# Attention 0 ahead of gate/up 0, and gate/up and projections in 64-row tile pairs with a shifted copy of x

## Chip, cores and metric

The kernel runs on one core of a Trainium2 chip. The metric is the device time of one execution in microseconds (us). The engines are called as in the profile: PE (matmuls; PEld its weight loads), DVE, ACT (functions such as exp, and copies), POOL, and SP, which issues most DMAs in one queue.

## What is computed

The input x has 2048 rows of 448 columns in bf16. Cut to what matters:

```python
xn = layernorm(x)
q, k, v = xn @ wq, xn @ wk, xn @ wv            # 16 heads of 28
for s in range(4):                             # segments of 512 rows
    p     = softmax(q_s @ k_s.T * 28**-0.5 + causal_mask)
    a_mem = phi(q_s) @ M / (phi(q_s) @ z + 1e-6)          # phi(t) = elu(t) + 1
    o_s   = g * a_mem + (1 - g) * (p @ v_s)               # g = sigmoid(beta), by head
    M, z  = M + phi(k_s).T @ v_s, z + phi(k_s).sum(rows)
s = o @ wo
g = silu((gelu(xn @ w_gate) * (xn @ w_up)) @ w_down)      # hidden width 1792
out = x + s * g
```

## The kernel before

`fast_path` (L339 to L1374) builds a list of operations, each with its engine, duration, buffers and dependencies. `arrange` (L276) then fixes the order on every engine once, when the program is built: it takes the operation that can start soonest, and among those near it the one of lowest priority number. Three tables steer it. `ORDER` (L273) is the sequence of stages; `PRIO` (L87 to L257) overrides priorities by name; `STEP` (L258 to L272) says behind which score step of its segment's attention an operation may stand. On the chip every engine runs its row in that order and waits for semaphores. SP's row is served in order too: a DMA that waits for its data holds those behind it.

The work is cut into segments of 512 rows and into stages. A(s) is attention of segment s, G(s) gate/up of segment s, D3 the last down-projection. Before, the sequence is G0, A0, A1, G1, A2, G2, A3, G3, D3.

*Layer norm and transposition.* x is normalised on DVE, ACT and POOL, and turned so that its 448 columns lie on partitions: three chunks of 128 and one of 64. Segment 0's two copies, a centred one for its projections and the normalised one for gate/up 0, are turned by PE (`turned_by_pe`, L590, transposes at L596), those of the other segments by transposing DMAs (L685).

*Projections.* A `Unit` is one block of 128 rows by one of q, k, v: three full 128-row matmuls and one of 64 rows (`product`, L711; L714 in the profile). `visit` (L768) collects the 64-row matmuls of several units: one unit uses the low 64 rows of the PE array, the next the high 64, so two run side by side. Results are copied out of PSUM by ACT or DVE (L750 to L754); q and k are turned by DMA (L763) into qT and kT. phi (L816) is exp on ACT (L826) and elementwise work on POOL and DVE.

*Attention.* Ten score steps per segment (L985) use 32-row tiles, four heads at a time. exp on ACT (L1000) reads one or two PSUM banks, POOL masks the diagonal blocks (L1011), P·V (L1047) uses tiles 32 columns wide. The denominators go through small DMAs: collected (L886), reshaped (L917), inverted, spread again (L926, L931), and multiplied in by POOL (L909, L948, L956). `read` (L898) and `update` (L860) are the linear memory. Between score steps PE gets other work: projections of a later segment, the down-projection of the segment before (L1155), and `wo` (L1185). The residual is L1176.

*Gate/up.* For each of 14 blocks of 128 hidden columns there are six full matmuls (L1089) and two of 64 rows (L1104), the latter collected over four blocks (`VISITS`): 

```python
VISITS = (((), (0, 1)), ((2, 3), (4, 5)), ((6, 7), (8, 9)), ((10, 11), (12, 13)))
for i, w in enumerate((wg_sb, wu_sb)):
    for c in range(NC3):                                   # NC3 = 3 chunks of 128 rows
        nc.tensor.matmul(out=bf[fc].ap(i), lhsT=w[:, c, fc * P:(fc + 1) * P], ...)
r = slice(i * HALF, (i + 1) * HALF)                        # gate low, up high
nc.tensor.matmul(out=bf[fc].ap(i), lhsT=wh_sb[r, fc * P:(fc + 1) * P], ...)
```

gelu is ACT's (L1114), the product with up DVE's (L1119); the result is hT, input of the down-projection. `guard` (L1239) checks a bound on the weights. `general_path` isn't run.

Of the kernel before, what the change touches and what calls it, by code (L numbers as in the profile page):

```python
# [1737 lines left out]
```

## Time and profile before

| what | value |
|---|---|
| time, median of 3 runs | 229.91 us (229.48 to 230.01) |
| span of the profiled execution | 228.8 us, 1.1 us below the median of the runs |
| PE busy | 219.1 us, 96% of the span |
| DVE, ACT, POOL busy | 152.5, 152.8, 129.2 us |
| granted clock of PE | full, 1.00 in nearly every stretch |
| DMA traffic | 25.09 MB, 110 GB/s on the mean |

The stages in that execution: the first gate/up matmul starts at 16.75 us, A0's first score at 39.29, A1's at 64.21, G1 at 89.39, A2 at 112.16, G2 at 139.76, A3 at 162.53, G3 at 187.11, the last down-projection at 209.99; PE's last large matmul ends at 223.1.

How to read the profile: a line such as `L1104 ... x4` is a group of four instructions of source line 1104; `ps` and `pp` are PSUM banks (single ones and pairs). "x3" behind a DMA transpose counts blocks. In the chain of waits each row is a piece of the path that ends last: its start, its length, and what ran. Of a stage, such a row tells which engine set its pace.

### The profile page before, as it was taken

The numbers are of one execution on the slowest core, as the hardware profiler recorded it, in microseconds if no ns is written. First come the engines' busy times: TensorE is split into PE (matmuls) and PEld (weight loads), VectorE is DVE, ScalarE is ACT, GpSimd is POOL, SyncE is SP. The second block draws the span as 40 slices with busy tenths as digits, with TensorE's granted clock in tenths as the row PEclk, the third lists the DMA queues.
The fourth block names the chain that finished last, engine by engine and source line by source line (L and its number), as shares of the span: only waits on it lengthen the run. The fifth ranks groups of instructions, "written<-read, shape, count | busy, mean of one in ns | idle before, by whom it ended". The sixth has DMA issues, their size and how long they took to land.

```text
span 228.8 us, 4476 instructions
## 1 busy us (share of the span) xinstructions
PE 219.1 (96%) x1570; PEld 95.8 (42%) x1570; DVE 152.5 (67%) x287; ACT 152.8 (67%) x212; POOL 129.2 (56%) x221
## 2 busy tenths in 40 slices
PE   7899999889999999999999999999999999999991
PEld 2444433334444444344444444444444434444570
DVE  3699998766955796674775587863836463548262
ACT  4699735999899679433788898443878875336020
POOL 8501400579579599602699989853198487604400
PEclk9999999999999999999999999999999999999999
DMA  6999559954436682326702122272400018133011
GB/s 211 230 354 253 103 129 251 251 116 92 52 72 72 177 130 53 80 52 191 197 20 59 35 70 62 66 195 84 114 1 4 11 44 227 34 103 99 4 40 47
DMA packets 44707, 25.09 MB, mean 110 GB/s; under 512 B 30808, under 2 KB 40856, under 8 KB 44680
## 3 DMA queue, kind: packets, MB, share of 16 engines
q1 hardware_dynamic: 43704, 24.05, 45.1%
q10 hardware_dynamic: 976, 0.71, 1.0%
q8 instruction: 13, 0.21, 0.4%
q14 instruction: 14, 0.11, 0.2%
HBM read 16.00 MB, written 2.98 MB: 83 GB/s over the span
## 4 chain that ended last, share of the span: by engine, by line
PE 83%; ACT 7%; DMA 4%; issue 2%; DVE 2%; ACTq 0%
PE ps L1089 16%; PE pp L1089 16%; PE ps L1155 14%; PE ps L714 11%; ACT pt L1000 6%; PE pp L985 5%; PE ps L1185 4%; PE ps L1047 3%; PE pp L1104 3%; PE ps L1104 3%; DMA wv_sb<-in_A_wv_dram 2%; PE pp L1155 2%; DMA qT<-e 2%; PE ps L898 1%; PE pp L714 1%
## 5 line engine op out<-in xcount | busy, mean ns | idle before, releaser
L1000 ACT ACTIVATE pt<-pp 128x1024 bf16<-128x1024 f32 x75 | 73.3, 1037 | 11.7 <-PE pp L985 9.8
L1011 POOL TENSOR_SCALAR_AFFINE_SELECT pt<-pt 128x256 bf16<-128x256 bf16 x128 | 54.0, 446 | 26.8 <-ACT pt L1000 24.4
L1155 PE MATMUL ps<-wd_sb,hT 128*128 128x448 bf16 x182 | 39.1, 354 | 0.4 <-DVE qs L750 0.4
L1114 ACT ACTIVATE gl<-pp 128x512 bf16<-128x512 f32 x28 | 15.8, 595 | 29.0 <-PE pp L1104 23.3
L1155 PEld LDWEIGHTS <-hT 128*128 128x128 bf16 x210 | 18.8, 98 | 20.0 <-issue 4.8
L1119 DVE TENSOR_TENSOR hT<-gl,pp 128x512 bf16<-128x512 bf16 x28 | 18.4, 682 | 12.3 <-ACT gl L1114 12.3
L1119 DVE TENSOR_TENSOR hT<-gl,ps 128x512 bf16<-128x512 bf16 x28 | 18.7, 677 | 10.7 <-ACT gl L1114 8.2
L1114 ACT ACTIVATE gl<-ps 128x512 bf16<-128x512 f32 x28 | 16.6, 597 | 13.2 <-PE ps L1089 6.7
L1089 PEld LDWEIGHTS <-wu_sb 128*128 128x128 bf16 x168 | 16.5, 98 | 20.0 <-issue 0.3
L1089 PEld LDWEIGHTS <-wg_sb 128*128 128x128 bf16 x168 | 14.9, 98 | 22.6 <-issue 6.8
L909 POOL TENSOR_TENSOR om<-om,rb 128x512 f32<-128x512 f32 x12 | 14.9, 1267 | 16.4 <-DMA rb<-rdr 16.4
L714 PEld LDWEIGHTS <-xnT 128*128 128x128 bf16 (+1 forms) x192 | 15.0, 96 | 20.9 <-issue 10.5
L1089 PE MATMUL ps<-xnT,wg_sb 128*128 128x512 bf16 x84 | 22.8, 380 | 0.0
L1089 PE MATMUL pp<-xnT,wg_sb 128*128 128x512 bf16 x84 | 22.8, 380 | 0.0
L1089 PE MATMUL ps<-xnT,wu_sb 128*128 128x512 bf16 x84 | 22.7, 379 | 0.1
L1089 PE MATMUL pp<-xnT,wu_sb 128*128 128x512 bf16 x84 | 22.7, 379 | 0.0
L956 POOL TENSOR_TENSOR oT<-oa,om 128x512 bf16<-128x512 f32 x12 | 16.0, 1341 | 11.0 <-DVE oa L953 11.0
L985 PE MATMUL pp<-qT,kT 32*128 32x512 bf16 (+3 forms) x238 | 17.3, 301 | 1.9 <-ACT pt L1000 1.8
L831 POOL TENSOR_SCALAR e<-e 128x896 bf16<-128x896 bf16 (+1 forms) x12 | 12.8, 1069 | 10.9 <-ACT e L826 10.9
L646 POOL TENSOR_TENSOR rs<-rs,nhalf 128x1 f32<-128x1 f32 (+1 forms) x7 | 6.1, 882 | 16.6 <-DVE rs L641 16.6
L883 DVE COPY oa<-ps 128x512 f32<-128x512 f32 x16 | 11.0, 684 | 6.0 <-PE ps L1047 5.5
L1176 POOL TENSOR_TENSOR oo<-sg,x_sb 128x448 bf16<-128x448 f32 x12 | 12.4, 1035 | 2.5 <-DVE sg L1196 2.5
(121 smaller groups left out, 326.0 us busy)
## 6 DMA issues: line engine op xcount, KB each, us to landing
rb<-rdr SPq DMA_DIRECT2D x28, 256.0 KB
out_dram<-oo SPq DMA_DIRECT2D x15, 112.0 KB
wd_sb<-in_B_w_down_dram SPq DMA_DIRECT2D x2, 784.0 KB
x_sb<-in_A_x_dram SPq DMA_DIRECT2D x3, 448.0 KB
rdr<-dc SPq DMA_DIRECT2D x28, 32.0 KB
wg_sb<-in_B_w_gate_dram SPq DMA_DIRECT2D x2, 384.0 KB
wu_sb<-in_B_w_up_dram SPq DMA_DIRECT2D x2, 384.0 KB
wg_sb<-in_B_w_gate_dram SPq DMA_DIRECT2D x1, 576.0 KB
```

Source lines behind the costliest of these rows:

```text
L714: nc.tensor.matmul(out=self.bank.ap()[:, 0:D], lhsT=self.xT.ap()[r, c, n * P:(n + 1) * P], rhs=self.w[r, c, :], **kw)
L831: o = gps(f"mi{nm}{s}{half}", n / 1024, lambda: nc.gpsimd.tensor_scalar(out=t(), in0=t(), scalar1=1.0, scalar2=0.0, op0=ALU.min, op1=ALU.max),
L909: oU[s, g, 1] = t, gps(f"sm{s}{g}", 1.22, lambda t=t, r=r: nc.gpsimd.tensor_tensor(out=t.ap(), in0=t.ap(), in1=r.ap(), op=ALU.mult), deps= ...
L956: oT[s][1].append(gps(f"cb{s}{g}", 1.22, lambda g=g, t=t, tm=tm: nc.gpsimd.tensor_tensor(out=dst.ap()[:, g, :], in0=t.ap(), in1=tm.ap(), o ...
L985: nc.tensor.matmul(out=S2[i // 2].ap(i % 2)[:, c0:c0 + n], lhsT=kT[s][0].ap()[r, g, kb * P:(kb + 1) * P], rhs=qT[s][0].ap()[r, g, kb * P:L ...
L1000: nc.scalar.activation(out=dst, in_=src, func=ACT.Exp, scale=scale)
L1011: nc.gpsimd.affine_select(out=v, in_=v, pattern=[[0, 2], [1, P]], compare_op=ALU.is_ge, fill=0.0, base=0, channel_multiplier=-1)
L1089: nc.tensor.matmul(out=bf[fc].ap(i), lhsT=w[:, c, fc * P:(fc + 1) * P], rhs=xT.ap()[:, c, :], start=begins and c == 0, stop=not begins and ...
L1104: nc.tensor.matmul(out=bf[fc].ap(i), lhsT=wh_sb[r, fc * P:(fc + 1) * P], rhs=xT.ap()[r, NC3, :], start=fc in begins, stop=fc in ends)
L1114: a = act(f"ge{s}{fc}", L, lambda: nc.scalar.activation(out=gl.ap(), in_=bf[fc].ap(0), func=ACT.Gelu_apprx_tanh), func="gelu", deps=[o], a ...
L1119: nc.vector.tensor_tensor(out=hT[s][0].ap()[:, fc, :], in0=gl.ap(), in1=bf[fc].ap(1), op=ALU.mult), deps=[a] + held,
L1155: nc.tensor.matmul(out=bank.ap()[:, 0:D], lhsT=hT[s][0].ap()[:, fc, b * P:(b + 1) * P], rhs=wd_sb[:, fc, :], start=(fc == 0), stop=(fc == ...
```

## The change

*Sequence.* `ORDER` becomes A0, G0, A1, G1, A2, G2, A3, G3, D3. Down-projection and residual of segment s - 1 now stand in A(s) for s = 1, 2, 3, and `combine` (the output of attention) of segment s behind G(s). Projections of segment 1 stand in A0; q and k of segment 2 in A1, its v in A2; q and k of segment 3 in A2, its v in A3. The tables `PRIO` and `STEP` are new; `STEP` now counts through all 40 score steps.

*64-row tiles throughout.* The 448 rows are cut into seven half chunks of 64 instead of 3 x 128 + 64. Gate weights lie in partitions 0 to 63 and up weights in 64 to 127 of one tensor, q and k weights likewise, and v weights twice. A block of gate/up is 14 matmuls of 64 rows, gate (low) and up (high) in turn, each into its own PSUM bank. A projection is a `pair` of units, 14 matmuls. `VISITS`, `full` and `halves` go.

*A shifted copy of x.* The low tile needs every half chunk of x in partitions 0 to 63, the high one in 64 to 127. What lies on the other side is read from a copy xS with the halves swapped. `swapped` makes it by two DMAs from on-chip memory to on-chip memory of 196 KB each, once per segment for the projections and once for gate/up; for the projections of segment 0 it comes from seven transposes by PE per block instead of four.

*Segment 0 and 1.* q and one block of k of segment 0 are turned by PE (20 transposes in all) and copied by ACT or DVE, the other three k blocks by DMA. The normalised x of segment 1 is turned by PE instead of DMA, that of segment 0 for gate/up 0 by DMA instead of PE.

*Buffers.* k, kT and v of segment 0 live in the down weights' tensor wd_sb, which is loaded after A0; qT of segment 0 lives in hT. x of segment 3 shares the tile of segment 0. The guard's squares go over the q/k tensor, behind A0.

The diff, cut to its core:

```diff
-ORDER = {"G0": 0, "A0": 1, "A1": 2, "G1": 3, "A2": 4, "G2": 5, "A3": 6, "G3": 7, "D3": 8}
+ORDER = {"A0": 0, "G0": 1, "A1": 2, "G1": 3, "A2": 4, "G2": 5, "A3": 6, "G3": 7, "D3": 8}
...
-        wg_sb = const.tile([P, NC3, F], BF16, name="wg_sb")
-        wu_sb = const.tile([P, NC3, F], BF16, name="wu_sb")
-        wh_sb = const.tile([P, F], BF16, name="wh_sb")
+        wgu_sb = const.tile([P, NH, F], BF16, name="wgu_sb")
...
+        def swapped(s, use, pr):
+
+            t, (xT, xd) = Buf(xS_p), xnT[s]
+            lo = dma(f"xs{use}{s}l", 196, lambda: nc.sync.dma_start(
+                out=t.ap()[side[0]], in_=xT.ap()[side[1], 0:NC3, :]), deps=list(xd), prio=pr, acq=[t], uses=[xT])
+            hi = dma(f"xs{use}{s}h", 196, lambda: nc.sync.dma_start(
+                out=t.ap()[side[1]], in_=xT.ap()[side[0], 1:NC3 + 1, :]), deps=list(xd), after=[lo], prio=pr, uses=[t, xT])
+            xS[s, use] = t, [lo, hi]
+
+        def chunk(xT, xt, h, hi):
+
+            if hi:
+                t, c = (xT, NC3) if h == 0 else (xT, h // 2) if h % 2 else (xt, h // 2 - 1)
+            else:
+                t, c = (xt if h % 2 else xT), h // 2
+            return t.ap()[side[hi], c, :]
+
+        turn_of = (0, 2, 4, 6, 1, 3, 5), (1, 3, 5, 0, 2, 4, 6)
...
-                r, n = slice(0, P) if c < NC3 else side[self.n % 2], self.n
-                nc.tensor.matmul(out=self.bank.ap()[:, 0:D], lhsT=self.xT.ap()[r, c, n * P:(n + 1) * P],
-                                 rhs=self.w[r, c, :], **kw)
+                h, n = turn_of[self.hi][k], self.n
+                nc.tensor.matmul(out=self.bank.ap()[:, 0:D], lhsT=chunk(self.xT, self.xt, h, self.hi)[:, n * P:(n + 1) * P],
+                                 rhs=self.w[side[self.hi], h, :], start=k == 0, stop=k == NH - 1)
...
+                    for k in range(NH):
                         for i in range(2):
+                            h = turn_of[i][k]
+                            nc.tensor.matmul(out=bf.ap(i), lhsT=wgu_sb[side[i], h, cols], rhs=chunk(xT, xt, h, i),
+                                             start=k == 0, stop=k == NH - 1)
+                o = prev = pe(f"gu{s}{fc}", [L] * 7, mm, mode="r64", deps=xd + xe + gu_in[fc],
+                              after=[prev or att.get("sc_end")], prio=at(ph, fc) + 0.5, acq=[bf], uses=[xT, xt])
...
-            d = max(s - 1, 0)
...
             if s > 0:
                 for b in range(NB):
-                    finish(d, b, at(A(s), 90 + 10 * b))
+                    down(s - 1, b, at(A(s), 12 + 24 * b))
+                for b in range(NB):
+                    finish(s - 1, b, at(A(s), 90 + 10 * b))
```

What stands on PE at the first scores of attention 0, before (kT and qT are keys and queries of segment 0, turned; L714 is a projection of segment 1):

```order
L1089 MATMUL ps_95<-xnT_98,wu_sb 128x512
L985 LDWEIGHTS kT_102
L985 MATMUL pp_91<-qT_100,kT_102 128x512
L985 LDWEIGHTS kT_102
L985 MATMUL pp_91<-qT_100,kT_102 128x512
L985 LDWEIGHTS kT_102
L985 MATMUL pp_90<-qT_100,kT_102 128x512
L985 LDWEIGHTS kT_102
L985 MATMUL pp_90<-qT_100,kT_102 128x512
L714 LDWEIGHTS xnT_99
```

And after (wd_sb holds the keys, hT the queries; L826 is the last projection of segment 0, with the shifted copy xS; L696 turns segment 1's x):

```order
L826 LDWEIGHTS xS_96
L826 MATMUL ps_88<-wv_sb,xS_96 128x448
L1097 LDWEIGHTS wd_sb
L1097 MATMUL pp_86<-hT,wd_sb 128x512
L1097 LDWEIGHTS wd_sb
L1097 MATMUL pp_86<-hT,wd_sb 128x512
L1097 LDWEIGHTS wd_sb
L1097 MATMUL pp_87<-hT,wd_sb 128x512
L1097 LDWEIGHTS wd_sb
L1097 MATMUL pp_87<-hT,wd_sb 128x512
L696 LDWEIGHTS xn_92
```

The scores moved from behind gate/up 0 to right behind the projections of segment 0.

PE at the start of gate/up 1, before (L1185 is the last `wo` of segment 0):

```order
L1185 MATMUL ps_92<-wo_sb,oT_126 128x448
L1104 LDWEIGHTS wh_sb
L1104 MATMUL ps_93<-xnT_99,wh_sb 128x512
L1104 LDWEIGHTS wh_sb
L1104 MATMUL ps_95<-xnT_99,wh_sb 128x512
L1104 LDWEIGHTS wh_sb
L1104 MATMUL pp_90<-xnT_99,wh_sb 128x512
L1104 LDWEIGHTS wh_sb
L1104 MATMUL pp_90<-xnT_99,wh_sb 128x512
L1089 LDWEIGHTS wg_sb
L1089 MATMUL ps_93<-xnT_99,wg_sb 128x512
```

And after:

```order
L1097 MATMUL pp_86<-qT_98,kT_100 128x128
L1195 LDWEIGHTS wgu_sb
L1195 MATMUL ps_88<-xnT_94,wgu_sb 128x512
L1195 LDWEIGHTS wgu_sb
L1195 MATMUL ps_90<-xnT_94,wgu_sb 128x512
L1195 LDWEIGHTS wgu_sb
L1195 MATMUL ps_88<-xnT_94,wgu_sb 128x512
L1195 LDWEIGHTS wgu_sb
L1195 MATMUL ps_90<-xnT_94,wgu_sb 128x512
```

Instead of four 64-row matmuls followed by full ones, 64-row ones follow one another, low and high in turn, and gate/up 1 stands behind the last scores of attention 1.

SP's row ahead of gate/up 0, after the change (xnT_95 is the normalised x of segment 0 and its second copy xS_96 the one that gate/up 0 reads; xnT_94 and xS_97 belong to segment 1):

```order
L870 DMA_TRANSPOSE wd_sb<-wd_sb 128x4x128 x3
L709 DMA xS_97<-xnT_94 64x1536
L711 DMA xS_97<-xnT_94 64x1536
L592 DMA wgu_sb<-in_B_w_gate_dram 64x7x512
L801 DMA_TRANSPOSE xnT_95<-xn_92 128x4x128 x2
L658 DMA wo_sb<-in_A_wo_dram 28x4x448 x3
L592 DMA wgu_sb<-in_B_w_up_dram 64x7x512
L801 DMA_TRANSPOSE xnT_95<-xn_92 128x4x128 x2
L870 DMA_TRANSPOSE qT_98<-qs 128x4x128
L592 DMA wgu_sb<-in_B_w_gate_dram 64x7x768
L870 DMA_TRANSPOSE qT_98<-e_103 128x4x128
L709 DMA xS_96<-xnT_95 64x1536
```

Before, the queue held at this place the transposes of k, q and x and the loads of x, wo and wd, and gate/up 0, which reads segment 0's x as PE turned it, waited for none of them.

More of the change, by code (lines that the diff above doesn't have):

```diff
@@ L493, in load, with weight @@
             return o
-        def weight(eng, name, dst, ap):
-            kb = ap.shape[1] / 4
-            return [load(eng, name, dst[:, 0:NC3, :], ap[0:NC3 * P, :].rearrange("(c p) n -> p c n", p=P), 3 * kb)
-                    ] + [load(eng, f"{name}{i + 2}", dst[i * HALF:(i + 1) * HALF, NC3, :], ap[NC3 * P:D, :], kb / 2, 110.0)
-                         for i in range(2)]
+        side = slice(0, HALF), slice(HALF, P)
+        def weight(eng, name, dst, hi, ap, parts):
+            v = ap.rearrange("(c p) n -> p c n", p=HALF)
+            return [load(eng, f"{name}{k or ''}", dst[side[hi], c, :], v[:, c, :], len(range(*c.indices(NH))) * ap.shape[1] / 8, 300.0)
+                    for k, c in enumerate(parts)]
         x0 = [load(e, f"x0{lo}", xs[0][:, lo:hi, :], x_v[0][:, lo:hi, :], 112 * (hi - lo))
@@ L503, in fast_path @@
         x_in = {0: [x0[0], x0[2], x0[1], x0[1]]}
[L504 to L508 removed]
+        even, odd = slice(0, NH, 2), slice(1, NH, 2)
+        wq_in, wk_in = [], []
+        for k in range(2):
+            wq_in += weight("ACT", f"wq{k}", wqk_sb, 0, A_wq, [(even, odd)[k]])
+            wk_in += weight("SP", f"wk{k}", wqk_sb, 1, A_wk, [(odd, even)[k]])
+        wqk_in = wq_in + wk_in
+        x_in[1] = [load("SP", "x1", xs[1][:], x_v[1], 448)] * NB
+        wv_in = weight("SP", "wvl", wv_sb, 0, A_wv, [slice(0, NH)]) + weight("SP", "wvh", wv_sb, 1, A_wv, [slice(0, NH)])
+        x_in[2] = [load("SP", "x2", xs[2][:], x_v[2], 448)] * NB
         gu_in = []
@@ L546, in fast_path @@
                 t[:, :, :, Dh:Dh + 1], 1.0), after=[o], prio=-389 + 300 * i))
-        ones_in = fill("POOL", "ones", 0.1, 20, ones[:], 1.0)
+        ones_in = [fill("POOL", f"on{i}{j}", 0.1, 20, ones[side[i], j:j + 1], float(i == j)) for i in range(2) for j in range(2)]
         bd_in = []
@@ L1124, in hidden @@
                 hT[s][1].append(m)
[L1125 to L1135 removed]
+            hT[s].append(prev)
             att["g_end"], att["gelu_end"] = prev, a
@@ L1241, in guard, with square, sums @@
             sq = [Buf(pt_p), Buf(pt_p)]
-            for n in range(2 * (NC3 + 1)):
-                i, c = divmod(n, NC3 + 1)
-                to, r, d = sq[n // 4], slice(0, P) if c < NC3 else side[0], Dh
-                w = (wk_sb if i else wq_sb)[r, c, :]
-                def square(n=n, to=to, r=r, d=d, w=w):
-                    nc.scalar.activation(out=to.ap()[r, n % 4, 0:H * d], in_=w, func=ACT.Square)
-                def sums(i=i, c=c, n=n, to=to, r=r, d=d):
+            for n in range(NH):
+                to = sq[n // 4]
+                def square(n=n, to=to):
+                    nc.scalar.activation(out=to.ap()[:, n % 4, 0:D], in_=wqk_sb[:, n, :], func=ACT.Square)
+                def sums(n=n, to=to):
@@ L1255, in guard, with both @@
                         after=[a], prio=pr, acq=[] if n % 4 else [to], uses=[to] if n % 4 else [])
-                last.append(dve(f"rq{n}", H * d / 960 + 0.05, sums, deps=[a], prio=pr, uses=[to]))
+                last.append(dve(f"rq{n}", D / 960 + 0.05, sums, deps=[a], prio=pr, uses=[to]))
             bank = Buf(B_, ONE)
-            o = pe("nrm", [128], lambda: nc.tensor.matmul(
-                out=bank.ap()[0:1, 0:2 * (NC3 + 1) * H], lhsT=ones[:],
-                rhs=um[:, 0, :], start=True, stop=True), deps=last + [ones_in], prio=pr,
-                acq=[bank])
+            def both():
+                for i in range(2):
+                    nc.tensor.matmul(out=bank.ap()[0:1, i * NH * H:(i + 1) * NH * H], lhsT=ones[:, i:i + 1],
+                                     rhs=red, start=True, stop=True)
@@ L1328, in fast_path @@
         last_block(at(8, 40))
-        for o in later:
-            o.after.append(xnT[1][1][-1])
+        for t, o in o_users:
+            t.users.append(o)
+        x_in[3][0].deps += [ops_by[f"fa0{b}"] for b in range(NB)]
         for s in range(NSEG):
```

417 lines of the change are left out of this document (188 added, 229 removed), and 457 rows, old and new, of tables (PRIO, STEP).

## The prediction

> **What bounds the kernel now.** I read the page's head first, then the busy time of each engine in eleven stretches cut at the starts of the stages, then the chain of waits, and last the timelines of ScalarE (ACT) and of the DMA queue (SPq) around attention 0. Page, engine totals and the chain's shares:
>
> ```profile
> span 228.8 us, 4476 instructions
> PE 219.1 (96%) x1570; PEld 95.8 (42%) x1570; DVE 152.5 (67%) x287; ACT 152.8 (67%) x212; POOL 129.2 (56%) x221
> PE 83%; ACT 7%; DMA 4%; issue 2%; DVE 2%; ACTq 0%
> ```
>
> TensorE (PE) is busy for 96% of the span and carries 83% of the chain. The other engines matter only where PE has a hole. The stretches show where (columns: stretch, its length, busy time of PE, PEld, DVE, ACT, POOL, granted clock, DMA share, GB/s):
>
> ```profile
> 0.00:16.75 16.75, 14.53 (x90) 7.08 (x92) 11.02 (x33) 11.72 (x26) 8.12 (x33) 1.00 0.89 262
> 16.75:39.30 22.55, 22.48 (x118) 8.90 (x114) 21.39 (x51) 14.91 (x25) 3.66 (x3) 1.00 0.86 185
> 39.30:64.20 24.90, 22.98 (x210) 9.77 (x211) 19.70 (x43) 23.30 (x29) 16.41 (x34) 1.00 0.66 126
> 64.20:89.40 25.20, 25.19 (x236) 11.09 (x237) 18.11 (x31) 21.57 (x27) 21.58 (x39) 1.00 0.59 104
> 89.40:112.20 22.80, 22.80 (x132) 9.21 (x132) 13.94 (x22) 10.84 (x17) 10.94 (x13) 1.00 0.49 127
> ...
> 223.10:228.80 5.70, 0.58 (x14) 0.43 (x11) 1.24 (x5) 0.56 (x2) 0.00 (x0) 0.92 0.18 47
> ```
>
> They are the start, gate/up 0, attention 0 (39.30), attention 1 (64.20), gate/up 1 (89.40), and the tail behind the last matmuls. From 64.20 on PE has no hole; before it, PE is idle at the start and in attention 0, and 5.7 us at the end hold almost no PE work. The clock is full, so it is no term. The pieces of the chain give PE's paces (start, us, what):
>
> ```profile
> 9.09 0.22 PE ps L596 x4
> 22.47 0.54 PE ps L1104 x4
> 23.01 0.43 PE pp L1104 x4
> 43.17 0.81 issue
> 43.98 5.35 ACT pt L1000 x8
> ...
> 57.55 3.62 DMA qT<-e
> 61.27 1.06 ACT e L826
> 74.17 0.33 PE pp L985 x8
> 81.64 0.66 PE ps L1047 x16
> 98.35 2.59 PE ps L1089 x12
> ```
>
> Twelve full 128-row gate/up matmuls take 2.59, so 0.216 us each. Four 64-row ones (L1104), which run as two pairs, take 0.43 when others of their kind stand ahead: a pair costs 0.216, as much as one full matmul. The same four take 0.54 right behind a full one: a change of tile shape costs 0.54 - 0.43 = 0.11 us. Eight 32-row score matmuls take 0.33, sixteen of P·V 0.66, four transposes 0.22 (0.055 each). In attention 0 the chain leaves PE: exp (L1000) for 5.35 us, then a transposing DMA and phi.
>
> **The change part by part.**
>
> *Tile shapes.* By the order of PE's instructions the work in columns stays: gate/up was 336 full matmuls and 56 pairs, 392 units, and is 784 halves, 392 pairs; projections were 144 + 24 = 168 units and are 168 pairs of 448 columns. What goes is changes of shape. I counted them in that order: 156 before, 112 after. Gate/up 1 to 3 have 10, 10 and 9 before and 3 each after; the rest is spread over gate/up 0 (7 to 3) and the attentions. That is 44 x 0.108 (the 0.11 above, unrounded) = **-4.75 us**. Added are 32 transposes: 20 for queries and keys of segment 0, 12 for shifted and later x: 32 x 0.055 = **+1.8 us**. Costing every instruction so, PE's sums are 213.8 before and 210.8 after. Before, 228.8 - 5.7 - 213.8 leaves 9.3 us in which PE did not progress.
>
> These are 4.8 at the start (16.75 against a sum of 11.96), 0.6 in gate/up 0 (22.55 against 21.96), 3.2 in attention 0 (24.90 against 21.7), 1.4 in all that follows to the last down-projection, and -0.7 there, where the sum is too high (13.8 for 13.1). The question is what each becomes.
>
> *Start.* PE's sum up to the first score is 11.95, as before up to the first gate/up; the loads ahead of it are again x and the three projection weights. I keep the 4.8 and add 0.25 for the last copy of transposed q and k: first score at 17.0, **+0.25**.
>
> *Attention 0* now follows directly, and PE's sum in it is only 16.7 (no down-projection exists yet to fill it). It is then a question of ACT and the queue.
>
> ```profile
> 10.47 0.63 ACT L752 ACTIVATE vaug<-ps,rs 128x448 bf16<-128x448 f32 x1 [1.87 <-POOL ones L525]
> 11.00 0.63 ACT L752 ACTIVATE vaug<-pp,rs 128x448 bf16<-128x448 f32 x1
> ...
> 39.30 1.28 ACT L1000 ACT_TABLE_LOAD   x1
> 44.93 1.96 ACT L1000 ACTIVATE pt<-pp 128x1024 bf16<-128x1024 f32 x2
> 46.74 1.13 ACT L1000 ACTIVATE pt<-ps 128x512 bf16<-128x512 f32 x2
> 47.70 2.01 ACT L1000 ACTIVATE pt<-pp 128x1024 bf16<-128x1024 f32 x2
> ...
> 52.27 1.08 ACT L826 ACTIVATE e<-kn 128x896 bf16<-128x896 bf16 x1
> 53.11 2.07 ACT L1000 ACTIVATE pt<-pp 128x1024 bf16<-128x1024 f32 x2
> ```
>
> From start to start two exps of 1024 columns take 46.74 - 44.93 = 1.81, 0.905 each; a score tile split into two of 512 takes 0.96; phi 0.84, a copy out of PSUM 0.53. Attention 0 has 17 + 3 of them, one phi and two operations of a copy's size (a copy, a square of the guard): 15.4 + 2.9 + 0.8 + 1.0 = 20.1 us of ACT. With the first exp at 17.6 the last ends at 37.7. Only the last scores, not the last exp, precede gate/up on PE: two score tiles can wait unread, and the last P·V stands behind 70 gate/up matmuls. So PE can go on some four exps earlier, at about 34. PE's own sum gives 17.0 + 16.7 = 33.7. Both lie below what the queue allows:
>
> ```profile
> 14.68 6.95 SPq L763 DMA_TRANSPOSE kT<-kn  x4
> ...
> 34.52 0.56 SPq L556 DMA_DIRECT2D wo_sb<-in_A_wo_dram  x1
> ...
> 48.88 1.21 SPq L763 DMA_TRANSPOSE qT<-e  x1
> 50.18 2.51 SPq L685 DMA_TRANSPOSE xnT<-xn  x2
> ```
>
> Gate/up 0 reads the shifted copy of x, made by two DMAs at the end of a row on SP: from about 17 on, behind one another, nine transposes (three kT, four xnT, two of the second group of queries), six loads and four shifting copies. At 1.25 a transpose (the 2.51 for two) and 0.5 to 0.56 for any other issue this is 11.3 + 3.4 + 2.0 = 16.7, the issue ends at 33.7. The 393 KB that the two move need 1.0 to 1.6 at 379 to 244 GB/s:
>
> ```profile
> 10.00:10.50 0.50, 0.50 (x6) 0.12 (x3) 0.42 (x2) 0.03 (x1) 0.38 (x5) 1.00 1.03 244
> ...
> 17.00:18.00 1.00, 1.00 (x7) 0.42 (x6) 1.00 (x2) 1.00 (x2) 0.10 (x1) 1.00 1.06 379
> ```
>
> I take the slow end, as weights move beside it: the copy lands at 35.3, gate/up 0 starts at 35.4. Attention 0 then lasts 18.4 for a sum of 16.7: its idle falls from 3.2 to 1.7, **-1.5**. The waiting DMAs hold what is queued behind them on SP: denominators and the next segment's keys, needed only after gate/up 0.
> [...] The rate that the profile shows for two 64-partition loads at once:
>
> ```profile
> 9.00:9.50 0.50, 0.50 (x7) 0.34 (x6) 0.15 (x1) 0.00 (x0) 0.50 (x2) 1.00 0.85 301
> ```
>
> That slice lies in wh_sb's two loads, one to the low and one to the high half of the partitions; at 301 GB/s the copies take 1.3, within my bounds. [...]
>
> *Gate/up 0* has its weights long before and no projection of keys beside it: the 0.6 goes, **-0.6**. If the weights' last parts, issued in the same row, are late, it costs up to that 0.6 again.
>
> *Attention 1 to 3.* Down-projection, residual and `wo` of the segment before fill PE there, and PE's sums are 26.4, 26.1 and 26.1, against 25.0, 27.5 and 23.7 before. Their waits were 1.4 us in all with gate/up 1 to 3. New is that POOL's work of a segment is crowded:
>
> ```profile
> L1011 POOL TENSOR_SCALAR_AFFINE_SELECT pt<-pt 128x256 bf16<-128x256 bf16 x128 | 54.0, 446 | 26.8 <-ACT pt L1000 24.4
> L948 POOL TENSOR_TENSOR oT<-oa,rb 128x512 bf16<-128x512 f32 x4 | 5.1, 1281 | 0.0
> L1176 POOL TENSOR_TENSOR oo<-sg,x_sb 128x448 bf16<-128x448 f32 x12 | 12.4, 1035 | 2.5 <-DVE sg L1196 2.5
> L831 POOL TENSOR_SCALAR e<-e 128x896 bf16<-128x896 bf16 x6 | 5.6, 934 | 10.9 <-ACT e L826 10.9
> ```
>
> Attention 1 has 32 masks (14.3), the four products for segment 0's output (5.1), four residuals (4.1) and about three phi (2.8 to 3.1): 26.5 of 26.4. Masks gate P·V; residuals and phi can slip into gate/up 1, where POOL was busy 10.94 of 22.8. I take 2.0 for the waits of all later stages in place of 1.4, **+0.6**; between 0.5 and 6 is possible.
>
> *The last down-projection and the tail* keep their work: 0. Guard, masks, buffer numbers and names: 0, hidden under PE's row; the guard's other squares lie in gate/up 0, where ACT was busy 14.91 of 22.55; without that cover they would cost some 6 x 0.53 = 3.2 us of ACT.
>
> Sum: -4.75 + 1.8 + 0.25 - 1.5 - 0.6 + 0.6 = -4.2, the span becomes 224.6. The profiled span is 1.1 below the median of 229.91 of three runs; with the same 1.1 the time is **225.7**.
>
> **The rivals.**
>
> *Slower: the DMA queue decides when gate/up 0 starts.* For it: under load four kT transposes took 6.95, 1.74 each, since each waits in the row for its copy by DVE, and the new row has nine, plus a shifted copy for segment 1 that waits in mid-row for that segment's x. Against it: 1.21 each at 48.88. At 1.74 the row is 9 x 0.49 = 4.4 longer, gate/up 0 starts at 39.8; with 2 us of waiting in mid-row at 41.8, and nothing on PE can run in its place, its order is fixed. Each us is a us: 225.7 + 6.4 = **232.1**. It decides (slower by over 0.3%) once gate/up 0 starts after 40.3.
>
> *No gain: POOL sets the attentions.* If masks, products and residuals interleave so that POOL is full at the 86% that it reached in attention 1 before (21.58 of 25.20), attention 1 takes 26.5 / 0.86 = 30.8, +4.4: **230.1**. For it: masks stand behind one-us products in POOL's row. Against it: residuals can slip.
>
> *Attention 0 at ACT's full durations.* If exps take their 1.037 mean rather than 0.905 from start to start, or copies and phi crowd ACT, the last scores come 13 x 0.13 = 1.8 to 3 later than 33.8 and pass the queue's 35.4 by up to 1.5; with another 1.0 in attention 1 to 3, **228.2**, still faster.
>
> *The change does not do what it says: long rows of 64-row pairs do not hold 0.216.* The longest such row in the profile is eight matmuls. Its weight loads:
>
> ```profile
> L1104 PEld LDWEIGHTS <-wh_sb 64*128 64x128 bf16 x112 | 4.3, 94 | 8.9 <-issue 5.8
> L1089 PEld LDWEIGHTS <-wu_sb 128*128 128x128 bf16 x168 | 16.5, 98 | 20.0 <-issue 0.3
> ```
>
> A half's load takes 94 ns against 98, so a pair has twice the loading of a full matmul, hidden if the two tiles load side by side. Four instructions must issue in 0.216, 54 ns each; P·V does 32 in 0.66, 21 ns each, so issue is no limit. Each 1% over 560 pairs is 1.2 us; at 3.5% the time is **229.9**, even.
> [...]
>
> **How the numbers follow.** A measurement of this kernel tells about 0.3%, 0.7 us, from no change: faster is below 229.2, slower above 230.6. Forecast 225.7 (own range 222.5 to 228): 0.58. ACT rival 228.2: 0.12. POOL rival 230.1: 0.08, half of it in "same". Queue rival 232: 0.15, nine in ten of it slower. Slow pairs: 0.07, spread evenly over the three. Faster 0.58 + 0.12 + 0.02 + 0.02 + 0.01 = 0.75, same 0.04 + 0.02 + 0.03 = 0.09, slower the remaining 0.16. The low end takes waits of zero after gate/up 0 and the queue as fast as PE (-2.0 - 1.7 = 222.0); the high end reaches into the queue rival, 231.0, so that under 2 in 10 lie outside.
>
> **What would show it.** Right: runs of 64-row pairs at 0.216; gate/up 1 to 3 within 22.6 each; first score near 17, gate/up 0 near 35.4, waiting for the shifted copy; no hole over 1 us later. Wrong: gate/up 0 after 40, PE waiting for a mask, twelve pairs above 2.65 us, or a first score after 19.

## The result: slower by 2.85%, and the profile after

The changed kernel takes **236.32 us**, the median of four runs (235.38 to 237.62), against 229.96 for the kernel before on the same chip: a ratio of 1.0285, 95% interval 1.0247 to 1.0323. The forecast was 225.7 with a range to 231.0; it is wrong, in sign too. The profiled execution has a span of 235.9 us and a time of 237.62, the longest of the four, 1.3 above their median. A few executions below ran over 1.5% longer than the fastest of their kernel; the ratios leave them out, while the times are medians of all. Page, engine totals and shares of the chain:

```profile
span 235.9 us, 5509 instructions
PE 219.2 (93%) x2084; PEld 102.8 (44%) x2084; DVE 157.3 (67%) x289; ACT 164.9 (70%) x224; POOL 130.3 (55%) x225
PE 74%; DMA 7%; SPq 5%; ACT 5%; DVE 4%; issue 2%; POOL 0%; DVEq 0%; ACTq 0%
```

PE is busy as long as before (219.1), so the 7.1 us that the span has grown by are idle time of PE. Its part of the chain fell from 83% to 74%, and the DMA queue (SPq), which had no share, has 5%. The stretches (columns as in the prediction) are the start, A0 (from 20.45), G0, and behind the dots the last down-projection and the tail:

```profile
0.00:20.45 20.45, 15.57 (x131) 8.78 (x132) 12.52 (x41) 13.05 (x26) 9.85 (x33) 1.00 1.13 197
20.45:42.22 21.77, 18.60 (x240) 8.88 (x239) 17.62 (x39) 18.37 (x23) 14.60 (x35) 1.00 0.91 165
42.22:67.57 25.35, 22.93 (x212) 10.29 (x212) 14.70 (x25) 18.04 (x28) 3.56 (x7) 1.00 0.95 173
...
216.07:229.86 13.79, 13.79 (x100) 8.35 (x100) 7.86 (x12) 4.78 (x9) 5.34 (x4) 1.00 0.20 51
229.86:235.90 6.04, 0.01 (x1) 0.00 (x0) 1.99 (x6) 0.25 (x1) 0.00 (x0) 0.69 0.17 45
```

PE's holes are in the first three rows: 4.9, 3.2 and 2.4 us. The last column and the one before it tell the other half: at the start the DMA engines are busy throughout (share 1.13) and move only 197 GB/s; before it was 0.89 and 262. Against the forecast's stages (that of G0 is 22.55 less 0.6, the two behind it follow from its sum), and with experiment e4, in which three waits for data are taken away:

| stretch | forecast | measured | excess | e4 |
|---|---|---|---|---|
| start, to the first score | 17.0 | 20.45 | +3.45 | 16.69 |
| A0 | 18.4 | 21.77 | +3.37 | 21.56 |
| G0 | 22.0 | 25.35 | +3.35 | 22.75 |
| A1 to G3 | 148.4 | 148.50 | +0.1 | 148.49 |
| last down-projection and tail | 18.8 | 19.83 | +1.0 | 20.01 |
| span | 224.6 | 235.9 | +11.3 | 229.5 |

The chain of waits names what stands in the holes (start, us, what):

```profile
3.17 8.81 DMA x_sb<-in_A_x_dram
12.00 1.69 DVE st L750 x3
...
18.06 0.40 DVE hT L847
18.60 0.38 PE pp L861 x4
...
51.80 6.56 DMA wgu_sb<-in_B_w_up_dram
...
98.46 3.02 PE pp L1195 x28
...
227.56 1.67 DMA out_dram<-oo
```

Segment 1's x lands only at 12.0. DVE then takes its statistics (`st`) and normalises it, and behind that in DVE's row stands the copy of a query block out of PSUM (hT, L847), which PE has to turn (L861) before the first score. The same view holds what the forecast got right: 28 matmuls of 64 rows, 14 pairs, take 3.02 us, 0.216 a pair. PE's waits up to 70 us (total, times, longest):

```profile
PE pp L1195 <- DMA xS<-xnT: 2.1, 2, 1.4
PE pp L1097 <- ACT pt L1112: 1.4, 3, 0.6
PE ps L1097 <- ACT pt L1112: 1.4, 1, 1.4
...
PE pp L861 <- DVE hT L847: 1.2, 1, 1.2
...
PE ps L826 <- DMA wv_sb<-in_A_wv_dram: 0.8, 1, 0.8
```

G0 waits 2.1 for the shifted copy xS, the turning of the last queries 1.2 for their copy, projections for weights; score matmuls (L1097) wait for exp (L1112). The DMA queue's own timeline has the two copies for G0 here:

```profile
36.37 1.67 SPq L870 DMA_TRANSPOSE qT<-e  x1
38.22 0.51 SPq L709 DMA_DIRECT2D xS<-xnT  x1
38.82 0.55 SPq L711 DMA_DIRECT2D xS<-xnT  x1
```

The forecast had their issue end at 33.7 and the data land 1.6 later. It ends at 39.4, and the last matmul that waits for them starts at 45.73, some 6 us behind the issue.

Last, how fast weights arrive, in slices of 2 us. Before:

```profile
12.00:14.00 2.00, 2.00 (x19) 0.98 (x18) 1.80 (x6) 2.00 (x5) 0.00 (x0) 1.00 1.03 334
14.00:16.00 2.00, 2.00 (x15) 1.09 (x13) 2.00 (x6) 2.00 (x6) 0.00 (x0) 1.00 1.07 359
16.00:18.00 2.00, 2.00 (x15) 0.72 (x14) 1.83 (x4) 2.00 (x5) 0.10 (x1) 1.00 1.08 384
```

And after:

```profile
8.00:10.00 2.00, 1.74 (x21) 1.06 (x20) 0.15 (x1) 0.01 (x1) 1.01 (x2) 1.00 1.14 238
10.00:12.00 2.00, 2.00 (x26) 1.07 (x25) 0.36 (x1) 1.52 (x4) 0.00 (x0) 1.00 1.14 211
12.00:14.00 2.00, 2.00 (x22) 1.54 (x18) 1.96 (x7) 2.00 (x5) 0.00 (x0) 1.00 1.14 198
```

The DMA engines count as full in both; they move 334 to 384 GB/s before and 198 to 238 after.

### The profile page after: what moved, and what is told of

Its sections match the earlier page's. It is cut to its first block, busy times and chain, and to the rows that moved or that the text cites. A ratio compares the mean times of both kernels' runs of the same rounds, so it can differ in the third digit from the quotient of the medians.

```text
span 235.9 us, 5509 instructions
## 1 busy us (share of the span) xinstructions
PE 219.2 (93%) x2084; PEld 102.8 (44%) x2084; DVE 157.3 (67%) x289; ACT 164.9 (70%) x224; POOL 130.3 (55%) x225
## 4 chain that ended last, share of the span: by engine, by line
PE 74%; DMA 7%; SPq 5%; ACT 5%; DVE 4%; issue 2%; POOL 0%; DVEq 0%; ACTq 0%
PE ps L1195 16%; PE ps L1231 16%; PE pp L1195 15%; PE ps L826 11%; PE pp L1097 5%; ACT pt L1112 4%; PE ps L1261 4%; PE ps L1159 4%; DMA x_sb<-in_A_x_dram 4%; SPq L870 3%; DMA wgu_sb<-in_B_w_up_dram 3%; PE ps L1010 1%; PE ps L972 1%; SPq L801 1%; DVE st L750 1%
## 5 line engine op out<-in xcount | busy, mean ns | idle before, releaser
L1112 ACT ACTIVATE pt<-pp 128x1024 bf16<-128x1024 f32 x75 | 73.1, 1028 | 15.5 <-PE pp L1097 15.3
L1195 PEld LDWEIGHTS <-wgu_sb 64*128 64x128 bf16 x784 | 38.7, 94 | 49.0 <-issue 4.9
L1231 PE MATMUL ps<-wd_sb,hT 128*128 128x448 bf16 x210 | 43.7, 353 | 0.0
L1195 PE MATMUL pp<-xnT,wgu_sb 64*128 64x512 bf16 x224 | 30.6, 376 | 0.4 <-DMA wgu_sb<-in_B_w_up_dram 0.3
L1195 PE MATMUL ps<-xnT,wgu_sb 64*128 64x512 bf16 x224 | 30.2, 376 | 0.0
L1021 POOL TENSOR_TENSOR om<-om,rb 128x512 f32<-128x512 f32 x12 | 14.8, 1263 | 21.5 <-DMA rb<-rdr 21.5
L1195 PE MATMUL pp<-xS,wgu_sb 64*128 64x512 bf16 x168 | 24.7, 376 | 2.1 <-DMA xS<-xnT 2.1
L1195 PE MATMUL ps<-xS,wgu_sb 64*128 64x512 bf16 x168 | 24.1, 376 | 0.0
L826 PE MATMUL ps<-wqk_sb,xnT 64*128 64x448 bf16 x116 | 15.2, 351 | 1.8 <-DMA wqk_sb<-in_A_wk_dram 1.1
L826 PEld LDWEIGHTS <-xnT 64*128 64x128 bf16 x192 | 8.9, 94 | 12.9 <-issue 6.3
L1097 PE MATMUL pp<-qT,kT 32*128 32x384 bf16 (+3 forms) x186 | 12.9, 300 | 0.2 <-ACT pt L1112 0.2
L1261 PE MATMUL ps<-wo_sb,oT 128*128 128x448 bf16 x52 | 11.7, 353 | 0.0
```

What stands on the lines that cost most here:

```text
L826: nc.tensor.matmul(out=self.bank.ap()[:, 0:D], lhsT=chunk(self.xT, self.xt, h, self.hi)[:, n * P:(n + 1) * P], rhs=self.w[side[self.hi], h ...
L1021: oU[s, g, 1] = t, gps(f"sm{s}{g}", 1.22, lambda t=t, r=r: nc.gpsimd.tensor_tensor(out=t.ap(), in0=t.ap(), in1=r.ap(), op=ALU.mult), deps= ...
L1097: nc.tensor.matmul(out=S2[i // 2].ap(i % 2)[:, c0:c0 + n], lhsT=kT[s][0].ap()[r, g, kb * P:(kb + 1) * P], rhs=qT[s][0].ap()[r, g, kb * P:L ...
L1112: nc.scalar.activation(out=dst, in_=src, func=ACT.Exp, scale=scale)
L1195: nc.tensor.matmul(out=bf.ap(i), lhsT=wgu_sb[side[i], h, cols], rhs=chunk(xT, xt, h, i), start=k == 0, stop=k == NH - 1)
L1231: nc.tensor.matmul(out=bank.ap()[:, 0:D], lhsT=hT[s][0].ap()[:, fc, b * P:(b + 1) * P], rhs=wd_sb[:, fc, :], start=(fc == 0), stop=(fc == ...
```

## The experiments

The theories, by the names that the expectations use. NARROW: a load into 64 partitions is slower per byte than one into 128, and since the change makes every load of projection and gate/up weights such a load, all that is queued early comes late. DVE ROW: the wait for segment 1's x, in DVE's row ahead of the query copy, sets the first score. QUEUE: it is the number and order of SP's issues. COUPLED: A0 is long because PE and ACT wait for each other over exp. PACE: PE itself, with its small waits for DVE, is slower in A0 than counted. Each was timed against the kernel before.

**e1, loads of 128 partitions.** Each weight tensor is filled as before, by loads over all partitions with the same bytes:

```diff
-            return [load(eng, f"{name}{k or ''}", dst[side[hi], c, :], v[:, c, :], ...)]
+            return [load(eng, f"{name}{k or ''}", dst[:, wr[0]:wr[1], :], ws[...].rearrange("(c p) n -> p c n", p=P), ...)]
...
-                "(c p) n -> p c n", p=HALF), ...
+                "(c p) n -> p c n", p=P) ...
```

> The changed kernel with all weights loaded by DMAs to 128 partitions instead of 64 (same bytes, same places in the queues, weights in other rows of the tensors, so the products are not the reference's). Theory NARROW (loads to 64 partitions run at little more than half the rate, 198 to 238 GB/s against 334 to 384 in the kernel before, and hold everything behind them): x of segment 1 lands near 8 instead of 12.0 us, the first score comes at about 17.5 instead of 20.45, gate/up 0 waits under 1 us instead of 2.1 for its shifted copy; time about 231, ratio to the kernel before 1.005. Rival QUEUE (the row of SP and the order of DVE set the start, whatever the rate): the first score stays within 1 us of 20.45, gate/up 0 within 1.5 of 42.2; time 234 to 236.

232.68 us, ratio 1.012 (1.0054 to 1.0185): 3.6 us less than the change. Rates and the first and third stretch of e1:

```profile
8.00:10.00 2.00, 2.00 (x28) 1.28 (x26) 1.15 (x3) 0.76 (x2) 0.76 (x2) 1.00 1.06 361
10.00:12.00 2.00, 2.00 (x25) 1.50 (x23) 1.90 (x8) 2.00 (x5) 0.00 (x0) 1.00 1.09 373
```

```profile
0.00:16.91 16.91, 14.41 (x131) 7.95 (x133) 11.70 (x40) 12.57 (x26) 8.16 (x33) 1.00 0.76 239
...
38.46:62.56 24.10, 22.74 (x212) 10.38 (x211) 14.54 (x25) 17.93 (x28) 3.57 (x7) 1.00 0.85 172
```

The rate is what it was before the change, the first score comes at 16.91 (forecast 17.0), and G0 no longer waits for xS; it is still 2.1 over its forecast, with waits of 1.3 in all for gelu, the product and up weights. NARROW holds, for the start wholly and for G0 in part. A0 stays at 21.55, and the time 1.7 above the expected 231.

**e8 and e9, the other way round, on the kernel before.** e8 splits each of its 128-partition weight loads into two of 64 partitions; e9, the control, makes the same number of loads but each over all partitions:

```diff
+ e8: dma_start(out=dst[z], in_=src[z]) for z in (slice(0, HALF), slice(HALF, P))
+ e9: dma_start(out=dst[:, z], in_=src[:, z]) for z in (slice(0, 1), slice(1, 3))
```

> The kernel before with every weight load of 128 partitions split into two of 64, low then high (same bytes, twice the issues, same result). NARROW: the rate over 8 to 18 us falls from 334 to 384 to about 210 GB/s, gate/up 0 starts 1 to 3 us later or waits inside for weights; time 232 to 236. If it is the issuing and not the partitions, the control below loses as much.

> Control for e8: the same loads split into as many DMAs, but each to 128 partitions (one chunk, then two). NARROW: rate over 8 to 18 us stays above 320 GB/s, time within 1 us of the kernel before (229.9). ISSUE rival: as late as e8.

e8 235.13, ratio 1.023 (1.0193 to 1.0267); e9 231.41, ratio 1.0063 (1.0031 to 1.0094). Slices of e8, then of e9:

```profile
12.00:14.00 2.00, 2.00 (x13) 0.93 (x11) 0.83 (x2) 0.00 (x0) 1.72 (x8) 1.00 0.95 230
14.00:16.00 2.00, 2.00 (x15) 0.96 (x12) 1.73 (x7) 1.61 (x4) 0.00 (x0) 1.00 1.12 243
```

```profile
12.00:14.00 2.00, 2.00 (x18) 0.89 (x17) 1.76 (x7) 2.00 (x6) 0.28 (x1) 1.00 0.93 242
14.00:16.00 2.00, 2.00 (x17) 1.20 (x16) 2.00 (x5) 2.00 (x6) 0.00 (x0) 1.00 0.97 306
16.00:18.00 2.00, 2.00 (x14) 0.72 (x13) 1.84 (x4) 2.00 (x5) 0.00 (x0) 1.00 0.99 328
```

In the kernel before, with nothing else of the change, narrow loads cost 2.3%, 5.2 us. Of that 3.7 (e8 less e9) come with the halved partitions, the rest with the additional issues. The first gate/up matmul starts at 20.51 in e8 and 17.07 in e9 (16.59 in the kernel before by the same view). The control missed its own expectation: it is 1.5 above the kernel before, not within 1, and its rate passes 320 GB/s only from 16 us on. Its loads that were of 64 rows from the start were issued at 7.4 to 9.8, which is likely why the slice from 12 to 14 is at 242; no run separates that.

**e2, no wait for segment 1's x.** Segment 1 is normalised from segment 0's x, which lies there early:

```diff
-                    out=st.ap(), in_=xs[s][:, b, :]), ...
+                    out=st.ap(), in_=xs[0 if s == 1 else s][:, b, :]), ...
```

> The changed kernel in which segment 1 is normalised from segment 0's x, already on the chip (values of segment 1 are not the reference's); order, sizes and loads as they were. DVE no longer waits for the load of segment 1's x ahead of copying q. Theory DVE ROW (that wait of 3.3 us stands on the chain to the first score): first score at about 18, gate/up 0 at about 40, time 233.5 to 234.5. Theory NARROW alone: the v weights still land at 16.3, so the first score moves by 1 to 2 us, and the weights and the shifted copy of gate/up 0 land as late as before; time 235 to 236.

237.59, ratio 1.0226 (1.0139 to 1.0313): no gain that could be told. The first score does come at 17.02, with the loads as narrow as before, so DVE ROW is right about its place; then PE's waits between 14 and 30 us have this row:

```profile
PE ps L1097 <- DMA wd_sb<-wd_sb: 3.4, 1, 3.4
```

The next score needs keys turned by three transposing DMAs (wd_sb to wd_sb), which stand in the slow queue behind the weights. One wait took the place of another, and the granted clock fell to 0.50 from about 22 to 31 us; of this profile only the places of the waits are read, not the lengths of the stages.

**e3, no shifted copy for G0.** G0 reads the unshifted x for all half chunks, and the two DMAs are left out:

```diff
+            lo = dma(f"xs{use}{s}l", 196, None if s == 0 and use == 'g' else lambda: ...
...
-                            nc.tensor.matmul(..., rhs=chunk(xT, xt, h, i),
+                            nc.tensor.matmul(..., rhs=chunk(xT, xt, h, i) if s else xT.ap()[side[i], h // 2, :],
```

> The changed kernel without the two DMAs of the shifted copy for gate/up 0, which reads the unshifted x instead (same matmuls, other values). If that copy is what gate/up 0 waits for: the 2.1 us of waiting go, time about 234.2. If the second half of the up weights, which landed at 58.36 with PE waiting 0.3 us, is late by itself: that wait grows by 1 to 2 us, and the time is 235 to 236.

235.49, ratio 1.0224 (1.0157 to 1.0291): 0.8 less than the change, with intervals that overlap. The xS wait is gone and G0 falls to 23.30, but in this run A0 grew to 23.83, with 2.2 of waiting for the transposed keys and a clock of 0.93; the wait for the up weights in G0 is 0.9 instead of 0.3. The copy's wait alone is not the price. Start and A0 trade with each other: e3 and e7 (below) load the start's data as the change does, and their first scores come at 18.34 and 19.72 instead of 20.45, yet G0 starts at 42.17 and 41.13, against 42.22. The split of the table's first two excesses is thus that of one execution. With wide loads (e1, e4, e10, e15, e16) the first score comes at 15.75 to 16.91 and G0 starts at 36.92 to 38.92.

**e4, e1 to e3 together.**

> The three edits together (128-partition loads, segment 1 normalised from segment 0's x, no shifted copy for gate/up 0). What is left is attention 0 in its new place with PE and ACT waiting for each other, and all that follows. NARROW and DVE ROW together: first score near 16, gate/up 0 near 37.5, no wait in it; time 227.5 to 229.5. If attention 0 itself is the cause, over 231.

231.74 (ten runs), ratio 1.0087 (1.0056 to 1.0119). A0 and G0:

```profile
16.69:38.25 21.56, 18.99 (x241) 8.94 (x240) 18.02 (x40) 18.64 (x24) 16.14 (x36) 1.00 0.86 167
38.25:61.00 22.75, 22.40 (x213) 11.13 (x213) 14.52 (x25) 17.82 (x28) 3.57 (x7) 1.00 0.78 172
```

Start and G0 are now near the forecast (16.69, 22.75). A0 is not: 21.56 for 18.4, and the time is over the 231 that the expectation gave for attention 0 as a cause of its own. PE is idle in it for 2.6 us, and busy for 18.99 where I had counted 16.7. A row of e4's chain, and A0 cut at its end, show how it adds up:

```profile
20.02 5.25 ACT pt L1112 x7
```

```profile
16.69:25.31 8.62, 6.40 (x68) 2.90 (x67) 5.81 (x17) 8.50 (x13) 4.46 (x10) 1.00 0.68 149
25.31:38.25 12.94, 12.59 (x173) 6.04 (x173) 12.21 (x24) 10.14 (x12) 11.68 (x28) 1.00 0.99 179
```

In the first 8.6 us ACT is full (8.50), seven exps stand on the chain, and PE is idle for 2.2; in the other 12.9 PE is full (12.59) and ACT is not (10.14). PE gets too little of its row done in the first part to finish earlier in the second.

**e5 and e10, half of A0's exp.** On e4, exp in A0 covers half the columns; the other half of its tiles is filled with ones by POOL, in e10 at an earlier place than in e5:

```diff
-                            nc.scalar.activation(out=dst, in_=src, func=ACT.Exp, scale=scale)
+                            nc.scalar.activation(out=dst[..., 0:L // 2] if s == 0 else dst, in_=src[..., 0:L // 2] if s == 0 else src, ...)
```

> The kernel of e4 (231.7 us; first score 16.7, gate/up 0 at 38.25) with the exps of attention 0 on half of their columns; the other half of each softmax tile is filled once with ones, so segment 0's attention is not the reference's. PE's row is the same. In e4 attention 0 lasts 21.6 us where PE's own sum is 16.7. Theory COUPLED (in the first 9 us PE has too little other work and waits for exp, in the rest ACT waits for PE; neither catches up): with exp at half the price PE's waits of some 3 us go, attention 0 lasts 18 to 18.5, time 228 to 229. Rival PE PACE (the tiles and changes of shape simply take longer than counted): attention 0 stays over 20.5, time over 230.8.

> The run of e5 again, with the softmax tiles filled with ones earlier on POOL, so that the fill does not delay segment 1's x and PE does not fall idle (in e5 PE's granted clock fell to 0.50 from 19.5 to 29.5 us, which hid the answer); segment 0's attention is not the reference's. COUPLED: attention 0 lasts 18 to 19 us instead of the 21.6 of e4, time 228 to 229.5 if the clock stays full. PE PACE: over 20.5 us at full clock.

e5 234.58, ratio 1.0129 (1.0077 to 1.0182): inconclusive, since the fill delayed segment 1's x, PE worked for only 1.0 of the 3 us from 17 to 20, and the granted clock was 0.50 from 19.5 to 29.5. e10 231.23, ratio 1.0085 (1.0055 to 1.0115), at full clock. Its A0:

```profile
16.47:36.92 20.45, 18.50 (x240) 8.75 (x239) 17.86 (x40) 11.55 (x24) 16.28 (x37) 1.00 0.86 174
```

ACT's work falls from 18.64 to 11.55, and A0 by 1.1 only, far from COUPLED's 18 to 19 and just under PACE's 20.5. Halved exps still hold PE for 0.7 us (1.6 in e4), so at least 1.1 of A0's excess of 3.2 hang on exp. From 23.79 to 27.59 e10's chain is then on DVE, with copies and sums in the place that e4's gives to exp:

```profile
21.17 0.61 ACT pt L1112
...
23.79 0.62 DVE kn L843
...
25.68 1.01 DVE wd_sb L956
```

Part of PACE can be read from e4's trace. Behind a wait the scores run two at a time, and two alone hold PE for 0.39 us, where the prediction had eight in 0.33 (the figure before PE is how long the row lasts, in brackets the idle time ahead of it):

```profile
21.58 0.39 PE L1097 MATMUL pp<-hT,wd_sb 32*128 32x512 bf16 x2 [0.29 <-ACT pt L1112]
22.50 0.39 PE L1097 MATMUL pp<-hT,wd_sb 32*128 32x512 bf16 x2 [0.53 <-ACT pt L1112]
```

I summed PE's time in A0 by source line, each matmul up to the start of the next. At the paces that the same lines have in the change's attention 1, where PE is busy for 27.50 of 27.70 us, and 0.055 a transpose, it would be some 17.3. The 1.7 above that are scores (0.8), projections (0.6) and transposes (0.3), broken up by the waits; the other 0.6 of the 2.3 is a count that was too low.

**e16, e10 with segment 1's projection copies on ACT** instead of DVE, to see whether DVE holds PE:

```diff
-                o = evict(f"ev{nm}{s}{n}", D, s == 0, put, ...
+                o = evict(f"ev{nm}{s}{n}", D, s == 0, put if s != 1 else lambda copy: put(nc.scalar.copy), ...
```

> e10 (half exps in attention 0 of e4, where it lasted 20.45 us against 21.6 with full exps and a counted 16.7) with the 12 copies of segment 1's projections out of PSUM moved from DVE to ACT, which the half exps leave free (attention 0 is not the reference's). If DVE, busy for nearly all of attention 0, is what PE waits for beside exp: 17.5 to 19 us, time 229 to 230. If PE's own pace is the rest: still over 20.

231.43, ratio 1.004 (0.9996 to 1.0083). A0 took 22.55, but the granted clock was 0.55 from 20 to 22 us and 0.60 from 22 to 24: inconclusive.

**e6, two queues.** The high halves of v's weights and of the first up weights are issued by ACT, beside the low halves that SP issues:

```diff
-(nc.sync if eng == "SP" else nc.scalar).dma_start(
+(nc.sync if eng == "SP" and name not in ("wvh", "wu0") else nc.scalar).dma_start(
```

> The changed kernel with the high halves of the v weights and of the first up weights issued by ACT beside the low halves from SP (same bytes and result). If a load to one half of the partitions reaches only part of the paths and the two halves together reach all: the rate over 10 to 18 us rises from 198 to 229 to over 280 GB/s, the v weights land near 14 instead of 16.3; time 234 to 235.5. If each load is slow by its own shape, the rate stays at 200 to 240, time 235.5 to 237.

235.66, ratio 1.0267 (1.0221 to 1.0312). The slices moved 228 to 239 GB/s between 8 and 14 us and 274 from 14 to 16, between the two expectations. The first score came at 17.70, but waits of 0.65 and 0.36 us followed it and the clock was 0.50 from 22 to 28: level with the change within the intervals.

**e7, an output tile for each of the last four blocks,** in the tile that held normalised x:

```diff
-                out=oo.ap()[:, r], in0=t.ap()[:, r], in1=xs[s][:, b, r], op=ALU.add), ...
+                out=(xn_p.aps[0][:, b] if s == LAST else oo.ap())[:, r], in0=t.ap()[:, r], in1=xs[s][:, b, r], op=ALU.add), ...
```

> The changed kernel with an output tile of its own for each of the last four blocks (in the tile that held normalised x), where two tiles took turns and DVE waited 1.55 us for an output DMA near the end. Same order, same result. If that wait is on the end's path: the time from the last gate/up matmul to DVE's last operation falls from 15.9 to 14.4 to 14.9, time about 1.2 us less than the changed kernel (235.1). If the last blocks' matmuls set the end anyway, it stays within 0.5.

It answers this row of the change, DVE at the end, where a block's sum waits until an earlier block's output has been stored and its tile is free:

```profile
229.32 0.32 DVE L1252 TENSOR_TENSOR oo<-sg,x_sb 128x160 bf16<-128x160 f32 x1 [1.55 <-DMA out_dram<-oo]
```

235.16, ratio 1.023 (1.0192 to 1.0269), 1.2 less than the change as expected, though the intervals overlap; the stage is clearer: from the last gate/up matmul to the last operation on DVE it is 14.8 us instead of 15.9 (14.6 in the kernel before). So the tail's excess is this wait. In this run G0's wait for xS was longer (2.7), and the slices of it (columns as above, PE first) show what that does:

```profile
43.00:44.00 1.00, 0.37 (x1) 0.09 (x1) 0.96 (x3) 1.00 (x3) 0.68 (x2) 1.00 2.92 138
44.00:45.00 1.00, 0.00 (x0) 0.00 (x0) 0.39 (x1) 0.98 (x2) 0.98 (x3) 0.62 0.06 6
...
50.00:51.00 1.00, 1.00 (x8) 0.45 (x6) 0.00 (x0) 0.00 (x0) 0.00 (x0) 0.50 0.64 129
51.00:52.00 1.00, 1.00 (x11) 0.44 (x8) 0.00 (x0) 0.01 (x1) 0.00 (x0) 0.96 0.64 130
```

**e11, loads later,** a version that might have won the time back: e7, with segment 2's x and the first gate and up weights behind the key transposes in SP's row, and the last up weights ahead of G0's copies:

```diff
+        for names, behind in [(('x2', 'wg0', 'wu0'), 'tk02'), (('wu8',), 'wg8')]:
+            ... order[at_k:at_k] = mv_ops
```

> The changed kernel, result unchanged, with SP's row in another order (x of segment 2 and the first gate/up weights behind the k transposes of segment 0, the last up weights ahead of the shifted copy for gate/up 0) and with an output tile of its own for each of the last four blocks. NARROW: fewer bytes stand ahead of what the start needs, so the v weights land 1 to 2 us earlier and k's transposes too; first score 18.5 to 20, end 1.2 us shorter; time 233 to 234.5. If it is DVE's order alone: the first score stays at 20 to 20.5, time 235.

240.15, ratio 1.0474 (1.0445 to 1.0503), where 233 to 234.5 had been expected. The first score came at 19.49, but the copies now land behind those loads. PE waits 1.7 us for them in A0's projections and 2.7 in G0.

**e12, queries first:** e11, with DVE's query copies ahead of segment 1's statistics, and that segment's transposes behind the first scores.

> As the run before, and DVE copies q of segment 0 and PE takes its scores ahead of segment 1's statistics and transposes, instead of behind them. DVE ROW: the first score no longer waits for segment 1's x (12.0) and comes at 17 to 18; but segment 1's projections, the only other work for PE in attention 0, come later, so attention 0 lasts 22 to 23; time 232 to 234. [...]

244.51, ratio 1.0661 (1.0617 to 1.0705), where 232 to 234 had been expected. The first score is at 17.00 as intended, and a moment later PE waits 3.6 us for segment 1's normalised x; from 20 to 29 us the granted clock is 0.50, and G0 waits 4.6 for xS.

**e15, e4 with e7's tiles,** all four costs taken away:

> e4 (128-partition loads, segment 1 normalised from segment 0's x, no shifted copy for gate/up 0; the output is not the reference's) with an output tile of its own for each of the last four blocks as well: all removable costs found so far taken away together. If they add up: 231.7 less 1.2, 230.3 to 230.8, level with the kernel before (229.9). If the change still had a hidden gain: under 229.

230.85 (ten runs), ratio 1.0005 (0.9968 to 1.0041): level with the kernel before. The four costs add up to the loss, and there is no net gain behind them. It shows where the time goes and is no kernel to use: it leaves out the copy that gate/up 0 needs, and the right x for segment 1.

## Why the prediction was wrong

**The start (+0.25): the step that failed first.** It said that the loads ahead of the first score "are again x and the three projection weights" and kept the 4.8 us of before. The bytes are nearly the same (v's weights come twice), the partitions they reach are not: 198 to 238 GB/s against 334 to 384, so segment 1's x came at 12.0 and the first score at 20.45. e1 gives 16.91 with wide loads. The lateness reaches the first score through DVE's row: without the wait for that x (e2) it comes at 17.02 even behind narrow loads, and the next wait, for keys, takes its place. The prediction asked for the rate into 64 partitions for the two shifting copies alone, and saw its bounds of 244 to 379 GB/s confirmed by a slice of 301 that it read as one load to the low and one to the high half together (e6, with such pairs, gave 228 to 274); it did not ask which other transfers had become 64 partitions wide, and these were all weights of the projections and of gate/up.

**Attention 0 (-1.5): too low by 3.4.** I took the largest of three sums, of PE (33.7), ACT (about 34) and the queue (35.4), for the end. With the loads' delays removed (e4) it is still 21.56 against 18.4. The step that failed is taking the largest sum over the whole stage: in e4 ACT is full in the first 8.6 us and PE in the 12.9 behind them, and such stretches add. Of the 3.2 us at least 1.1 hang on exp (e10), which is the ACT rival's mechanism. In e4 PE is idle for 2.6 us (1.6 of it for exp, 0.7 and 0.2 for DVE's copies) and busy for 2.3 more than counted, most of that in rows that these waits break up. The count was low before, too: PE was busy for 22.98 in attention 0, and the prediction took the 1.3 above its sum of 21.7 for idle time, which it then let shrink. How much of the rest is DVE's is not settled: e16, meant to tell, was disturbed by its clock.

**Gate/up 0 (-0.6): +3.35.** It waits 2.1 for the shifted copy and 0.3 for weights; the other 0.9 is PE's own work, 22.93 for 22.0. That the queue decides when gate/up 0 gets on was the rival at 0.15, with 232.1; place and sign were its own. Its price, issue time, was only part: the issue ended at 39.4 and not at 33.7 (3.45 of it the later start), and then the data took 6 us to land instead of 1.6. With wide loads (e1) the wait is gone, though the row of issues is the same.

**Tile shapes (-4.75 + 1.8) and later stages (+0.6): right.** Pairs ran at 0.216 in rows of 28, A1 to G3 took 148.50 for 148.4. G1 to G3 took 22.6 to 22.8. The rivals on POOL and on slow pairs did not occur. That the later stages meet the forecast so closely is in part luck: attention 1 took 27.70 for a counted 26.4, and behind 67 us PE's waits come to 0.2 where 2.0 had been allowed.

**The tail (0): +1.0,** from two output tiles that the last blocks now wait for (e7). I had taken "keep their work" to mean the same time.

**The time outside the span.** In every execution on record with its span, the time is 1.7 to 1.9 us above it. The prediction added 1.1, the distance from one execution's span to a median of three times; by 1.7 it would have said 226.3.

**The clock.** In the three other runs of the change its mean was 0.985 to 0.988, against 0.989 to 1.000 in the runs of before. The forecast held it full. It explains none of the stages above: the profiled run, the longest, had 0.992, with 1.00 in each stretch but the tail.

That the loss is these waits and not the pairs is shown by e15: without all four the span is 229.1, 6.8 below the change's and level with before, with the pairs as they are. The 4.5 over the forecast that stay there lie in A0 (22.25 for 18.4) and G0 (24.13 for 22.0), less 1.25 by which the first score came earlier; G0's waits there are 0.7 for up weights and 0.7 for gelu and the product. Not tried: gate/up in pairs without any shifted copy.

## What to carry to other kernels

When a change alters the shape of a tensor on chip, price every load into it by the partitions that it reaches and not by its bytes alone (198 to 238 GB/s into 64 here, 334 to 384 into 128), and then ask what is queued behind it. A stage in which several engines hand work to each other in a fixed order can take longer than the largest of their sums: attention 0 did (21.56 for 18.4 in e4), while attentions 1 to 3, where the down-projection fills in, kept PE busy (27.50 of 27.70 us, 26.44 of 26.44 and 26.36 of 26.36). So split such a stage where the limiting engine changes, and add. Moving one wait away was worth little here (0.8 at most in e3, none in e2, a loss in e11 and e12), because another stood right behind it.
